# An attention and MoE kernel on one core: a fixed table of places for the first 820 operations, and another form of load for the second batch's queries

## The chip, the core and the metric

The kernel runs on one core of one Trainium2 chip. Its time is the device time of one execution in microseconds (us); the kernel before has a median of 866.38 us over three runs (864.64 to 868.58). The engines are PE (TensorE, with PEld for its weight loads), DVE (VectorE), ACT (ScalarE), POOL (GpSimd) and SP (SyncE), which here issues every DMA. Each engine works through its own instructions in the order in which the program has them; an instruction that waits holds up all that stand behind it on its engine.

## What is computed

```python
def _attn_ref(q, k, v):                        # q, k, v: 8 batches, 8 heads, 576 tokens, 64
    q_s = np.exp(q - np.max(q, axis=-1, keepdims=True))
    q_s = q_s / (np.sum(q_s, axis=-1, keepdims=True) + 1e-09)      # softmax over the 64
    k_s = np.exp(k - np.max(k, axis=2, keepdims=True))
    k_s = k_s / (np.sum(k_s, axis=2, keepdims=True) + 1e-09)       # softmax over the tokens
    kv = np.einsum('bhsd,bhse->bhde', k_s, v)
    return np.einsum('bhsd,bhde->bhse', q_s, kv)
...
x = attn_out.transpose(0, 2, 1, 3).reshape(4608, 512)
h = x @ w_in                                   # 512 x 2048
g = h * (1.0 / (1.0 + np.exp(-1.702 * h)))
out = g @ w_out                                # 2048 x 512
```

## The kernel before

The 4,608 tokens are cut into 12 tiles `t` of 384 (`TB`), three tokens to each of the 128 partitions. A batch has 576 tokens, so that tile 0 lies in batch 0, and tile 1 takes the last 192 tokens of batch 0 (on partitions 0 to 63) and the first 192 of batch 1 (on partitions 64 to 127). In float32 throughout, a product is made of three matmuls: each factor is split into a high part (`xh`, `gh`) and a low part (`xl`, `gl`).

**Attention.** `load_q`, `load_k`, `load_v` and `load_tail` load queries, keys, values and the last 64 tokens of keys and values, four heads (`i` = 0 or 1) at a time. `k_max` and `k_sub` make the keys' exponentials, `q_soft` the queries' softmax (DVE maximum L751, subtraction L755, ACT exponential L759, DVE sum L763, product L771 into `en`), `widen` (L428) copies the values, `kv_pairs` (PE L663) makes kv, `q_tr` (PE L793) transposes the queries, `x_pairs` (PE L876, L881) makes the attention's output x, and `x_out` (ACT L841, L853, PE L851, DVE L844) splits it. Batches 0 and 1 land in tiles of their own: `eq0`, `ek0`, `ev0`, `et` and `eq1`, `ek1`, `ev1`, `kl`, `vl`.

**MoE of tiles 0 and 1.** The loop runs over 16 slices `j` of the hidden layer. `g1` (PE L906, 12 matmuls of 128x384) makes h, ACT the gelu (L912) and its high part (L915), DVE the low part (L918), and `g2` (PE L938, nine matmuls of 128x512) adds to the output, which stays in PSUM. The weights come in as they are needed: `load_w` loads a slice or a pair of slices of `w_in` (`wi`, L316) or `w_out` (`wo`, L321), and `conv_w` (ACT L349 and L364, DVE L353, L357, L374) splits it.

**MoE of tiles 2 to 11.** They run in pairs as a Strassen-like product: seven products (`product`, PE L1180) and six parts of the output (`out_part`, PE L1244) for each step, with weights that `store` wrote to DRAM and `refill` brings back.

**What sets the order.** No loop of the program does. `Plan.add` records 2,604 operations with their engine, an assumed cost, what they read and write, and a rank; loads have a size as well. `Plan.order` then plays the program through with those assumed costs: an engine that is free takes the ready operation with the lowest rank, and loads share one wire of `RATE` bytes per us and land `LAND` us after it. The order in which operations begin is the order in which they are written out. The first 820 operations (those with a rank under `LIMIT`: attention of the first tiles, all weight loads, the MoE of tiles 0 and 1 and the first steps towards tiles 2 and 3) have their ranks replaced by the list `FIRST`, one number each:

```python
begun = [n for n, o in enumerate(plan.ops) if o[3] < LIMIT]
for n, r in zip(begun, FIRST):
    e, cost, deps, _, run, table, size = plan.ops[n]
    plan.ops[n] = e, cost, deps, r / 100, run, table, size
```

For the prediction these places matter: on SP the order of the loads (L519 queries, L439 keys, L453 values, L416 and L419 tails, L316 and L321 weights); on DVE and ACT the chains of `q_soft` for batch 1 between the steps that make x of tile 0; and on PE the first `g1` (L906), with which the MoE begins.

Of the kernel before, what the change touches and what calls it, by code (L numbers as in the profile page):

```python
# [17 lines left out]
class Plan:  # L18
# [4 lines left out]
    HOP, LAND, RATE, ISSUE, TABLE = 0.1, 2.2, 330e3, 0.6, 1.28  # L23
# [25 lines left out]
    def order(self):  # L49
        ops = self.ops  # L50
        left = [len(o[2]) for o in ops]
        users = [[] for _ in ops]
# [7 lines left out]
        at = [0.0] * len(ops)  # L60
# [7 lines left out]
        while len(began) < len(ops):  # L68
# [4 lines left out]
            for e in engines:  # L73
                if free[e] > now or not ready[e]:
                    continue
                _, n = heapq.heappop(ready[e])
                _, cost, _, _, _, needs, size = ops[n]
                if needs is not None and needs != table:
                    cost, table = cost + self.TABLE, needs
                free[e] = done = now + cost  # L80
                if size:
                    wire = max(wire, done) + size / self.RATE
                    done = wire + self.LAND
                began.append(n)
                self.start[n] = now
                moved = True
                for u in users[n]:
                    left[u] -= 1
                    hop = 0.0 if ops[u][0] == e and not size else self.HOP
                    at[u] = max(at[u], done + hop)  # L90
                    if not left[u]:
                        heapq.heappush(coming, (at[u], u))
# [76 lines left out]
def efficient_attention_then_gelu_ffn(  # L169
# [137 lines left out]
    def load_w(j, kind, rank):  # L307
# [16 lines left out]
        plan.add("SP", n * plan.ISSUE, (), (*keys, ("loaded", tags[0])), rank, run, size=n * 2 * DM * 4 * P)  # L324
# [82 lines left out]
    def load_tail(b, rank):  # L407
# [13 lines left out]
        plan.add("SP", plan.ISSUE, behind(b == 2), (keys[0],), rank, run_k, size=ST * H * D * 4)  # L421
# [1109 lines left out]
```

## Time and profile before

| what | value |
| --- | --- |
| median of three runs | 866.38 us (864.64 to 868.58) |
| the profiled execution's own time | 865.18 us |
| its span, first to last instruction | 863.4 us |
| PE busy (matmul), PEld | 838.8 us (97%), 735.5 us (85%) |
| DVE busy, ACT busy | 468.1 us (54%), 464.3 us (54%) |
| granted clock of PE, mean | 0.995 |
| DMA moved | 191.81 MB, mean 222 GB/s |

PE is busy for 97% of the span, which is a mean over stages: the views by stage stand in the prediction. A row of the timeline gives start, duration, engine, line, operation, tiles and, in brackets, how long the engine had been idle before it and what ended that. A row of the chain of waits gives start, duration and what the chain ran through. A row of the table of stretches gives the stretch and its length, then for PE, PEld, DVE, ACT and POOL the busy time and number of instructions, then the clock that PE was granted (1.00 is full), the mean busy share of the 16 DMA engines, and what they moved.

### The profile page before, as it was taken

The page shows a single profiled execution, that of the slowest core. Times are in us where ns is not written, and L with a number is a line of the kernel's source. Part 1 is how long each engine was busy: PE and PEld are TensorE (multiplying, and loading weights), DVE is VectorE, ACT ScalarE, POOL GpSimd, SP SyncE. Part 2 cuts the span into 40 slices and gives each one's busy share as a digit, 9 for nine tenths or more (in the row PEclk, how much of TensorE's full clock was granted, in tenths as well). Part 3 has the DMA queues.
Part 4 walks back from the last instruction along what each step waited for, and adds up shares of the span by engine and source line. Part 5 has one row for each costly group of instructions (what it writes and reads, how often), then busy time and mean ns, then how long its engine had stood idle before and what let it go on. Part 6 is the DMA issues. An engine that isn't in the chain of part 4 may idle for free.

```text
span 863.4 us, 12622 instructions
## 1 busy us (share of the span) xinstructions
PE 838.8 (97%) x4822; PEld 735.5 (85%) x4822; DVE 468.1 (54%) x791; ACT 464.3 (54%) x773; POOL 18.6 (2%) x21
## 2 busy tenths in 40 slices
PE   3799999999999999999999999999999999999998
PEld 2489998888888889888988888889888889888897
DVE  6789678886746573634476445557432434312212
ACT  6788558665536584564375465377423535423332
POOL 1000000000000000000000000000000000000000
PEclk9999999999999999999999999999999999999999
DMA  9997989729776658769547559656665455654522
GB/s 283 295 384 269 351 325 338 189 75 255 269 273 219 224 197 259 239 196 293 194 158 257 188 180 267 225 179 211 220 199 162 165 195 197 220 207 161 191 102 74
DMA packets 134924, 191.81 MB, mean 222 GB/s; under 512 B 65872, under 2 KB 97104, under 8 KB 134864
## 3 DMA queue, kind: packets, MB, share of 16 engines
q1 hardware_dynamic: 134864, 191.01, 68.2%
q8 instruction: 38, 0.62, 0.3%
q14 instruction: 22, 0.18, 0.1%
HBM read 154.21 MB, written 36.77 MB: 221 GB/s over the span
## 4 chain that ended last, share of the span: by engine, by line
PE 92%; DMA 4%; DVE 1%; SPq 1%; ACT 1%; issue 0%; POOL 0%; DVEq 0%; POOLq 0%
PE bank L1244 39%; PE bank L1180 33%; PE bank L938 8%; PE bank L906 7%; PE bank L793 2%; PE bank L881 2%; PE bank L663 2%; DMA eq<-in_q 1%; DMA ev<-in_v 1%; DMA kt<-in_k 1%; DMA ek<-in_k 1%; PE bank L876 1%; SPq L453 0%; SPq L1353 0%; DVE qm L763 0%
## 5 line engine op out<-in xcount | busy, mean ns | idle before, releaser
L1180 PE MATMUL bank<-xc,w 128*128 128x384 f32 x960 | 184.2, 337 | 0.0
L1180 PEld LDWEIGHTS bank<-xc,w 128*128 128x128 f32 x960 | 170.7, 188 | 8.6
L1244 PE MATMUL bank<-w,gp 128*128 128x512 f32 (+1 forms) x633 | 172.5, 396 | 0.0
L1180 PE MATMUL bank<-w 128*128 128x384 f32 x720 | 137.7, 337 | 0.4 <-DVE g L1196 0.4
L1244 PEld LDWEIGHTS bank<-w,gp 128*128 128x128 f32 x633 | 116.1, 188 | 24.9 <-issue 3.9
L1180 PEld LDWEIGHTS bank<-w 128*128 128x128 f32 x720 | 127.7, 188 | 3.8 <-DVE g L1196 0.7
L1244 PE MATMUL bank<-w,gh 128*128 128x512 f32 (+1 forms) x326 | 103.6, 399 | 0.0
L1244 PE MATMUL bank<-w 128*128 128x512 f32 x324 | 93.4, 396 | 0.0
L1215 ACT COPY bank<-bank 128x384 f32<-128x384 f32 x40 | 18.5, 463 | 129.1 <-PE bank L1180 129.1
L906 PE MATMUL bank<-xh,w 128*128 128x384 f32 x256 | 70.2, 339 | 0.0
L1244 PEld LDWEIGHTS bank<-w 128*128 128x128 f32 x324 | 59.8, 188 | 11.7 <-issue 0.6
L1244 PEld LDWEIGHTS bank<-w,gh 128*128 128x128 f32 x326 | 59.1, 188 | 12.1 <-issue 3.2
L1244 PE MATMUL bank<-w,gl 128*128 128x512 f32 (+1 forms) x163 | 64.0, 392 | 0.0
L938 PE MATMUL bank<-w,gh 128*128 128x512 f32 x192 | 62.2, 405 | 0.0
L906 PEld LDWEIGHTS bank<-xh,w 128*128 128x128 f32 x256 | 46.8, 188 | 2.2 <-issue 0.6
L1215 ACT COPY g<-bank 128x384 f32<-128x384 f32 x40 | 19.2, 479 | 49.5 <-PE bank L1180 49.3
L1215 ACT COPY work<-bank 128x384 f32<-128x384 f32 x40 | 19.2, 479 | 46.3 <-PE bank L1180 46.2
L906 PE MATMUL bank<-xl,w 128*128 128x384 f32 x128 | 43.2, 337 | 0.0
L938 PEld LDWEIGHTS bank<-w,gh 128*128 128x128 f32 x192 | 35.7, 191 | 5.6
L1211 DVE TENSOR_TENSOR gp<-work,gp 128x384 fp32r<-128x384 f32 x35 | 19.3, 555 | 35.0 <-ACT gp L1208 35.0
L938 PE MATMUL bank<-w,gl 128*128 128x512 f32 x96 | 38.1, 397 | 0.0
L1211 DVE TENSOR_TENSOR gp<-g,gp 128x384 fp32r<-128x384 f32 x35 | 19.7, 562 | 32.3 <-ACT gp L1208 32.3
(157 smaller groups left out, 1118.3 us busy)
## 6 DMA issues: line engine op xcount, KB each, us to landing
w<-dwo SPq DMA_DIRECT2D x80, 512.0 KB, 4.9
w<-dwi SPq DMA_DIRECT2D x44, 512.0 KB, 3.4
w<-dsh SPq DMA_DIRECT2D x32, 512.0 KB, 3.9
w<-dsl SPq DMA_DIRECT2D x32, 512.0 KB, 5.3
raw<-in_moe_w_in SPq DMA_DIRECT2D x16, 512.0 KB, 9.9
raw<-in_moe_w_out SPq DMA_DIRECT2D x16, 512.0 KB, 9.9
dwi<-w SPq DMA_DIRECT2D x16, 512.0 KB, 6.2
dwo<-w SPq DMA_DIRECT2D x16, 512.0 KB, 5.9
```

Source lines behind the costliest of these rows:

```text
L663: nc.tensor.matmul(pk[r0 : r0 + D, m, :], lhs, rhs, start=c == 0, stop=c == CM, tile_position=(0, r0))
L793: nc.tensor.transpose(pq[:, c * P : (c + 1) * P], qt[:, c, o : o + 2, :], ident)
L876: nc.tensor.matmul(po, kx, qx, start=True, stop=True)
L881: nc.tensor.matmul(po[ro], kx[ri, ro], qx[ri], start=fresh, stop=True, skip_group_check=True, tile_position=((a ^ odd) * D, a * D),)
L906: nc.tensor.matmul(ph, wi[w][j][:, c, :], x[:, c, :], start=c == 0 and i == 0, stop=c == KC - 1 and i == 2,)
L938: nc.tensor.matmul(po[c], x[:, cs], wo[w][j], start=j == 0 and i == 0, stop=j == NJ - 1 and i == 2)
L1180: nc.tensor.matmul(pb, ws[w][:, c * P : (c + 1) * P], xx[x][:, c * TB : (c + 1) * TB], start=p in FRESH and c == 0 and i == 0, stop=c == 1 ...
L1211: lambda: nc.vector.tensor_tensor(out=get()[1], in0=d, in1=get()[0].bitcast(F32), op=ALU.subtract),
L1215: plan.add("ACT", act(TB), (PB,), (key,), early_, lambda: nc.scalar.copy(dst, pb))
L1244: nc.tensor.matmul(po[:, f0:f1], x[:, cs], w[:, h * DM + f0 : h * DM + f1], start=m == 0 and e == 0 and i == 0, stop=m == NQ - 1 and e == ...
```

## The change

There are three parts.

**A table of places.** `FIRST` now holds the numbers 0 to 819, one place for each of the first 820 operations. They are sorted by it, and `order` gets the sorted list: of two operations on the same engine that follow each other in the list, the second may not begin before the first has. So each engine takes these operations in exactly the table's order. All other operations are still taken by rank whenever their engine is free and they are ready.

**Second batch's queries.** `load_q` for tile 1 loaded, for each half `i`, two blocks of 64 partitions by four heads by 192 values (one from batch 0, one from batch 1). Now it loads one head at a time over all 128 partitions, four loads for each half: the source is an access pattern written out by hand with two blocks of 64 rows (the step from the first to the second leads from batch 0's token 384 to batch 1's token 0 of the same head).

**Sizes and rates of the plan.** `RATE` rises from 330e3 to 395e3 and `LAND` falls from 2.2 to 2.1; the assumed size of `w_in`, keys and values grows by 1.17, that of queries by 1.1, tails have 1.8 of one tail's bytes each, and the two small loads of the identity three times theirs. These numbers only steer the order of the operations.

```diff
-    HOP, LAND, RATE, ISSUE, TABLE = 0.1, 2.2, 330e3, 0.6, 1.28
+    HOP, LAND, RATE, ISSUE, TABLE = 0.1, 2.1, 395e3, 0.6, 1.28
...
+        last, chain = {}, {}
+        for n in first:
+            e = ops[n][0]
+            if e in last:
+                chain[last[e]] = n
+                left[n] += 1
+            last[e] = n
...
-                for u in users[n]:
+                after = [(u, done + (0.0 if ops[u][0] == e and not size else self.HOP)) for u in users[n]]
+                if n in chain:
+                    after.append((chain[n], now))
+                for u, when in after:
                     left[u] -= 1
-                    hop = 0.0 if ops[u][0] == e and not size else self.HOP
-                    at[u] = max(at[u], done + hop)
+                    at[u] = max(at[u], when)
...
 FIRST = [
-    5378, -14100, -14622, -13398, -9246, -12627, -7965, -8342, -15809, -12626, -10477, -6145, -11454, -5989,
...
+    641, 3, 2, 4, 16, 12, 35, 5, 1, 0, 6, 22, 19, 14, 32, 42, 77, 34, 46, 24, 65, 87, 40, 74, 60, 69, 99, 80,
...
+            if t == 1:
+                for h in range(n):
+                    src = q[0:1, n * i + h, TB:S, :].rearrange("b (p c) d -> b p (c d)", c=C)
+                    step = [(H * S - TB) * D, 2]
+                    src = bass.AP(src.tensor, src.offset, [step, *list(src.ap)[1:]])
+                    nc.sync.dma_start(out=qt[:, h].rearrange("p c d -> p (c d)"), in_=src)
+                return
...
-    for n, r in zip(begun, FIRST):
+    first = sorted(begun, key=lambda n: FIRST[begun.index(n)]) if FIRST else []
+    for place, n in enumerate(first):
         e, cost, deps, _, run, table, size = plan.ops[n]
-        plan.ops[n] = e, cost, deps, r / 100, run, table, size
+        plan.ops[n] = e, cost, deps, place - 1e5, run, table, size
...
-        for n in plan.order():
+        for n in plan.order(first):
```

The line numbers in the changed program are other ones: L519 and L525 are loads of queries, L438 of keys, L452 of values, L414 and L417 of tails, L313 and L318 of weights; L757 to L777 is `q_soft`, L847 and L859 `x_out`, L912 `g1`.

**SP, the loads after the first batch's keys and values.** Before, the order of the loads from the eleventh on was this:

```order
L416 DMA kl0_107<-in_k 64x8x64
L321 DMA raw_218<-in_moe_w_out 128x1024
L439 DMA ek1_124<-in_k 128x4x256
L316 DMA raw_223<-in_moe_w_in 128x4x256
L453 DMA ev1_126<-in_v 128x4x256 x2
L419 DMA vl0_108<-in_v 64x8x64
L439 DMA ek1_124<-in_k 128x4x256
L321 DMA raw_235<-in_moe_w_out 128x1024
L519 DMA eq1_125<-in_q 64x4x192 x2
L316 DMA raw_247<-in_moe_w_in 128x4x256 x2
L519 DMA eq1_125<-in_q 64x4x192 x2
```

In the changed program stands there:

```order
L318 DMA raw_213<-in_moe_w_out 128x1024
L417 DMA et_129<-in_v 64x8x64
L313 DMA raw_219<-in_moe_w_in 128x4x256
L452 DMA ev0_123<-in_v 128x4x256
L519 DMA eq1_125<-in_q 128x1x192 x4
L438 DMA ek1_124<-in_k 128x4x256 x2
L313 DMA raw_265<-in_moe_w_in 128x4x256
L414 DMA kl0_107<-in_k 64x8x64
L519 DMA eq1_125<-in_q 128x1x192 x4
L313 DMA raw_293<-in_moe_w_in 128x4x256 x2
L452 DMA ev1_126<-in_v 128x4x256
```

The second batch's queries (`eq1`) come before its keys and values (`ek1`, `ev1`) and in eight loads instead of four; the first batch's keys and values (`ek0`, `ev0`) stay ahead of them, in both.

**ACT, the stretch in which x of tile 0 is finished.** Before, from the first of the last two `qT` on (the transposed queries; `xh0` and `xl0` are the high and low part of x of tile 0):

```order
L806 ACTIVATE qT2_101<-bank3_66,rb0_191 128x384
L853 CAST xl0_77<-bank0_63 128x384
L584 ACTIVATE ek1_124<-ek1_124 128x1024
L585 ACTIVATE kl0_107<-kl0_107 64x256
L841 CAST xh0_76<-bank3_66 128x384
L841 CAST xh0_76<-bank5_68 128x384
L853 CAST xl0_77<-bank3_66 128x384
L853 CAST xl0_77<-bank5_68 128x384
L759 ACTIVATE eq1_125<-eq1_125 128x768
L584 ACTIVATE ek1_124<-ek1_124 128x1024
L585 ACTIVATE kl0_107<-kl0_107 64x256
```

Now, up to the last `xl0`, the whole stretch from the first exponential of the second batch's queries on:

```order
L765 ACTIVATE eq1_125<-eq1_125 128x768
L705 COPY kvn0_74<-bank7_70 64x2x64
L347 ACTIVATE work0_84<-raw_265 128x512
L812 ACTIVATE qT2_101<-bank3_66,rb0_191 128x384
L812 ACTIVATE qT3_102<-bank4_67,rb0_191 128x384
...
L847 CAST xh0_76<-bank3_66 128x384
L362 CAST w_391<-work0_84 128x512
L859 CAST xl0_77<-bank3_66 128x384
L765 ACTIVATE eq1_125<-eq1_125 128x768
L347 ACTIVATE work2_86<-raw_293 128x1024
L859 CAST xl0_77<-bank5_68 128x384
```

Both exponentials of `eq1` and the conversion of a pair of `w_in` slices now stand ahead of the last `xl0`; the first `g1` reads all of `xh0` and `xl0`. The exponentials of `ek1`, one of which stood ahead, come after.

**DVE, the second half of those queries.** In the changed program these rows follow each other (`qm2` is the maximum over 64 values, L757 takes it, L761 subtracts it):

```order
L757 TENSOR_REDUCE qm2_195<-eq1_125 128x12
L559 TENSOR_TENSOR mx0_105<-tmp0_93 128x256
L355 SCALAR_TENSOR_TENSOR work0_84<-work0_84,raw_265 128x512
L562 TENSOR_TENSOR mx0_105<-mx0_105,kl0_107 64x256
L761 TENSOR_TENSOR eq1_125<-eq1_125,qm2_195 128x768
```

Before, the two halves' maxima stood after all keys of batch 1 had their maximum, with the steps of the other half between them:

```order
L751 TENSOR_REDUCE qm2_195<-eq1_125 128x12
L672 TENSOR_SCALAR rb1_192<-bank3_66 128x2
L673 RECIPROCAL rb1_192<-rb1_192 128x2
L755 TENSOR_TENSOR eq1_125<-eq1_125,qm2_195 128x768
L763 TENSOR_REDUCE qm3_196<-eq1_125 128x12
```

A conversion of weights (L355) and two steps of the keys' maximum moved in between the queries' maximum and subtraction.

More of the change, by code (lines that the diff above doesn't have):

```diff
@@ L47, in add, with order @@
         self.ops.append((engine, cost, deps, rank, run, table, size))
-    def order(self):
+    def order(self, first=()):
         ops = self.ops
         left = [len(o[2]) for o in ops]
+        last, chain = {}, {}
[5 more added lines that the diff above has]
+            last[e] = n
         users = [[] for _ in ops]
@@ L323, in load_w @@
         keys = [(tag, x) for tag in tags for x in (0, "v")]
-        plan.add("SP", n * plan.ISSUE, (), (*keys, ("loaded", tags[0])), rank, run, size=n * 2 * DM * 4 * P)
+        size = n * 2 * DM * 4 * P * (1.17 if kind == "wi" else 1)
+        plan.add("SP", n * plan.ISSUE, (), (*keys, ("loaded", tags[0])), rank, run, size=size)
     nt, nwork = [0], [0]
@@ L419, in run_v @@
             nc.sync.dma_start(out=vl[0:ST, :, 0:D], in_=v[b, :, SM:S, :].rearrange("h p d -> p h d"))
-        plan.add("SP", plan.ISSUE, behind(b == 2), (keys[0],), rank, run_k, size=ST * H * D * 4)
-        plan.add("SP", plan.ISSUE, behind(b == 2), (keys[1],), rank + 0.01, run_v, size=2 * ST * H * D * 4)
+        size = 1.8 * ST * H * D * 4
+        plan.add("SP", plan.ISSUE, behind(b == 2), (keys[0],), rank, run_k, size=size)
+        plan.add("SP", plan.ISSUE, behind(b == 2), (keys[1],), rank + 0.01, run_v, size=size)
     def widen(b, i, rank):
@@ L442, in run @@
             )
-        plan.add("SP", plan.ISSUE, behind(b == 2), (key,), rank, run, size=n * SM * D * 4)
+        plan.add("SP", plan.ISSUE, behind(b == 2), (key,), rank, run, size=1.17 * n * SM * D * 4)
     def load_v(b, i, rank):
@@ L463, in load_v @@
         if b < 2:
-            plan.add("SP", plan.ISSUE, (), (key,), rank, run, size=n * SM * D * 4)
+            plan.add("SP", plan.ISSUE, (), (key,), rank, run, size=1.17 * n * SM * D * 4)
             vbuf[b, i] = vt_[i], ("vt", i)
@@ L528, in load_q @@
         plan.add(
-            "SP", plan.ISSUE * len(parts(t)) * len(runs),
+            "SP", plan.ISSUE * (n if t == 1 else len(parts(t)) * len(runs)),
             behind(1 < t < EARLY_T) + after + (LOADED if t == EARLY_T else ()), (key, *alloc), rank, run,
-            size=n * TB * D * 4,
+            size=1.1 * n * TB * D * 4,
         )
@@ L1353, in ident_in @@
         nc.sync.dma_start(out=ident, in_=dident.rearrange("p f -> (p f)")[: P * P].rearrange("(p f) -> p f", p=P))
-    at(-100, lambda rank: plan.add("SP", plan.ISSUE, (), ("dident",), rank, ident_out, size=P * P * 4))
-    at(-89.2, lambda rank: plan.add("SP", plan.ISSUE, ("dident",), ("ident",), rank, ident_in, size=P * P * 4))
+    at(-100, lambda rank: plan.add("SP", plan.ISSUE, (), ("dident",), rank, ident_out, size=3 * P * P * 4))
+    at(-89.2, lambda rank: plan.add("SP", plan.ISSUE, ("dident",), ("ident",), rank, ident_in, size=3 * P * P * 4))
     at(-89.1, lambda rank: plan.add("ACT", act(P), ("ident",), ("minus",), rank, lambda: nc.scalar.mul(minus_r, ident, -1.0)))
```

88 rows, old and new, of the table FIRST are left out of this document.

## The prediction

> **What bounds the kernel now.** The page gives the whole first:
>
> ```profile
> span 863.4 us, 12622 instructions
> PE 838.8 (97%) x4822; PEld 735.5 (85%) x4822; DVE 468.1 (54%) x791; ACT 464.3 (54%) x773; POOL 18.6 (2%) x21
> ```
>
> PE lacks 24.6 us of the span. The table of stretches says where (columns: stretch, length, busy time of PE, PEld, DVE, ACT, POOL, granted clock, DMA share, GB/s):
>
> ```profile
> 10.00:20.00 10.00, 5.70 (x50) 4.52 (x51) 8.09 (x17) 6.63 (x12) 1.06 (x1) 1.00 1.11 308
> 20.00:30.00 10.00, 7.56 (x62) 4.08 (x61) 8.98 (x19) 8.77 (x18) 1.06 (x1) 0.96 1.11 298
> 30.00:40.00 10.00, 9.04 (x70) 6.82 (x70) 6.50 (x10) 6.43 (x13) 1.06 (x1) 0.87 1.10 284
> 40.00:50.00 10.00, 7.09 (x63) 6.18 (x64) 8.29 (x17) 7.83 (x16) 0.00 (x0) 0.83 1.06 386
> 50.00:60.00 10.00, 10.00 (x55) 9.06 (x55) 9.10 (x15) 9.89 (x17) 0.00 (x0) 1.00 1.04 387
> ...
> 220.00:863.00 643.00, 639.77 (x3567) 563.53 (x3565) 295.88 (x512) 311.93 (x535) 8.27 (x7) 1.00 0.62 204
> ```
>
> From 50 us on PE is full; the 3 us lacking after 220 are the usual seams, and neither part of the change touches them. What the change can move is the first 50 us, where PE waits and where the DMA engines never do: their share is above 1.0 from 10 us on, so all sixteen have packets in the queue all the time, and what lands later in the queue lands later by the price of what lands ahead of it. In the head the chain of waits (start, duration, what) runs through exactly these loads:
>
> ```profile
> 15.40 9.66 DMA ev<-in_v
> ...
> 26.09 10.98 DMA eq<-in_q
> ...
> 41.89 0.97 DVE en L771
> ...
> 42.91 1.54 PE bank L793 x6
> ```
>
> and three moments of the timeline show what it costs there:
>
> ```profile
> 33.68 0.69 PE L663 MATMUL bank<-vt,ek 128*64 128x65 f32 x16
> 33.78 0.48 ACT L853 CAST xl<-bank 128x384 fp32r<-128x384 f32 x1 [0.15 <-PE bank L851]
> ...
> 35.00 0.45 PE L906 MATMUL bank<-xh,w 128*128 128x384 f32 x1
> ...
> 42.91 1.33 PE L793 MATMUL bank<-ident,en 128*128 128x128 f32 x5 [3.48 <-DVE en L771]
> ```
>
> The first `g1` begins at 35.00, straight after `kv_pairs` of batch 1 (33.68 to 35.00, 1.3 us). The last `xl0` that it needs was there at 34.26. It works until 42.91 - 3.48 = 39.43, so 4.4 us, and then stops for 3.48 us for `en`, the queries of tile 1, whose second half is the load that ends the 10.98 us, at 37.07. So the end follows from a simple sum: all PE work from the first `g1` on is given, and the end is the **start of the first `g1`**, plus this work, plus what PE idles behind that start (3.48 us).
>
> **The change, part by part.** The plan's sizes and rates cost the chip nothing; they act through the order alone. Whether the table is obeyed is seen in the order rows above: it is. What remains is how the loads are made and what now stands ahead of the first `g1`.
>
> *The price of a new load.* What before pays for queries:
>
> ```profile
> eq<-in_q SPq DMA_DIRECT2D x2, 384.0 KB, 4.3
> eq<-in_q SPq DMA_DIRECT2D x4, 192.0 KB, 9.9
> ...
> 18.70 0.43 DVE L353 TENSOR_SCALAR raw<-raw 128x512 uint32<-128x512 uint32 x1 [0.20 <-DMA raw<-in_moe_w_out]
> ```
>
> Half of tile 1's queries is 384 KB (393,216 bytes), formerly two loads of 64 rows, now four of 128. Bytes alone don't set the price: the stretches with the 64-row loads move 284 and 298 GB/s, the one from 40 to 50, in which only 128-row loads of weights go, 386. No load in the trace is written like the new one. Every load of before has an outermost dimension of 64 or more on both sides, and its stretches show sixteen busy engines. The new one's source is two blocks, each of 64 rows: its outermost dimension is 2. So the cost is bounded from both sides. If the sixteen engines share it, half the queries cost 393,216 / 386e3 = 1.0 us to 393,216 / 298e3 = 1.3 us. If the rows are dealt out by the outermost dimension, two engines carry it all. One engine moves 386/16 = 24.1 to 308/16 = 19.3 GB/s; 393,216 bytes over two take 8.2 to 10.2 us (11.1 at 284). By rows alone the price is anywhere from 1.0 to 11.1 us, and the nearest row, the 64-row load, lies at the cheap end. I nevertheless take the dear end, 9.2 us, the mean of 8.2 and 10.2, since the outermost dimension is the one thing in which these loads differ from all that use sixteen engines.
>
> The Trainium skill bears on this, "DMA: Bandwidth & Descriptors", section "Why a DMA increments its semaphore by 16 and not by 1": a transfer uses the largest number of engines up to 16 that divides the slowest dimension over 1 on either side, as the instruction carries it. For 2 and 128 this is two engines, the dear end; by any sharing over sixteen it would be the cheap one. The loads of before, all multiples of 16 there, agree with their DMA share of 1.06 to 1.11; the case of two engines no run here shows.
>
> *When the queries land.* In before the first `wo` has landed by 18.70. Ahead of the new loads stand the same loads without `kl` (128 KB, 0.4 us at 308 GB/s; as a 64-row load more, I take 0.8), so they begin at **17.9**. First half: 17.9 + 9.2 = 27.1. Then `ek1` twice, a `w_in` slice and `kl`, 1.70 MB, 4.4 us at 386 and 5.5 at 308 GB/s, taken as 5.0: 32.1. The two engines have their sixteenths of these to carry as well, so being alone saves them nothing. Second half: **41.3** (38.7 with all quick ends, 45.6 with 11.1 and 5.5). SP has four more issues to make; at 0.96 us (one in before's chain, wait included) that is 3.8 us, and it runs 9.9 us ahead of the landing, so this hides; if it didn't, 3.8 us would be the price.
>
> *What stands behind them.* The groups by line, operation and shape (busy, mean ns of one | idle before it):
>
> ```profile
> L751 DVE TENSOR_REDUCE qm<-eq 128x12 f32<-128x768 f32 x4 | 3.8, 946 | 6.7 <-DMA eq<-in_q 6.7
> L755 DVE TENSOR_TENSOR eq<-eq,qm 128x768 f32<-128x768 f32 x4 | 3.8, 949 | 0.1
> L553 DVE TENSOR_TENSOR mx<-tmp 128x256 f32<-128x256 f32 x16 | 6.7, 422 | 0.3
> L556 DVE TENSOR_TENSOR mx<-mx,kl 64x256 f32<-64x256 f32 x14 | 5.7, 415 | 0.6 <-DMA kl<-in_k 0.2
> L357 DVE SCALAR_TENSOR_TENSOR work<-work,raw 128x512 int32<-128x512 int32 x4 | 2.8, 689 | 0.6 <-ACT work L349 0.5
> L759 ACT ACTIVATE eq<-eq 128x768 f32<-128x768 f32 x4 | 3.4, 845 | 1.6 <-DVE eq L755 1.6
> L349 ACT ACTIVATE work<-raw 128x1024 f32<-128x1024 f32 x14 | 15.9, 1152 | 0.9 <-ACT w L364 0.9
> L853 ACT CAST xl<-bank 128x384 fp32r<-128x384 f32 x4 | 1.9, 476 | 0.2 <-PE bank L851 0.2
> L428 ACT COPY vt<-ev 128x1024 f32<-128x1024 f32 x4 | 4.2, 1053 | 2.5 <-DMA ev<-in_v 2.5
> L584 ACT ACTIVATE ek<-ek 128x1024 f32<-128x1024 f32 x3 | 3.2, 1056 | 0.0
> L585 ACT ACTIVATE kl<-kl 64x256 f32<-64x256 f32 x14 | 5.6, 401 | 0.0
> ```
>
> From the second half's landing on DVE does, in the order of the rows above, maximum, L553, L357, L556 and subtraction: 0.95 + 0.42 + 0.69 + 0.42 + 0.95 = 3.43 us. ACT then has the exponential, the conversion of a `w_in` pair and the last `xl0`, which stand in a row: 0.85 + 1.15 + 0.48 = 2.48. With 0.2 us of hops the first `g1` starts at 41.3 + 3.4 + 2.5 + 0.2 = **47.4**. Nothing shortens this: each engine keeps its order, and tile 0's x, long since computed by PE, waits behind tile 1's queries.
>
> *The sum.* First `g1` 35.0 to 47.4: +12.4. `kv_pairs` of batch 1 now comes behind it: +1.3. The wait of 3.48 for `en` goes: before, the last `en` ended 5.8 us after its landing (42.86 - 37.07), now with the two steps between some 7.3 later, at 48.6, and PE has `g1` until 47.4 + 4.4 = 51.8: -3.5. What is late next is the stalls behind the new start, none to 2.5 us (gelu, keys and values of batch 1, which land after 41); I take 1.3. Sum **+11.5**, bounds from +7.6 (38.7, no stall) to +17.0 (45.6, 2.5). The half clock neither gains nor loses:
>
> ```profile
> 43.00:46.00 3.00, 3.00 (x11) 2.61 (x12) 2.90 (x4) 2.64 (x7) 0.00 (x0) 0.50 1.07 394
> ```
>
> After its 3.48 us of idling PE is granted 0.50 for some 3 us, which costs 1.5; behind the longer wait of the new kernel the same is due once.
>
> The profiled execution took 865.18 us and the median is 866.38, 1.2 more. So 865.2 + 11.5 = 876.7 for the profile, and **877.9** for the median, own range 874 to 883.
>
> **Rivals.** *A: sixteen engines share the new loads, and the table does what it is for* (not slower). Landings: 17.9 + 1.2 = 19.1 and, 5 + 1.2 us later, 25.3. The second half is then 11.8 us sooner than at 37.07, and no `en` is waited for. ACT sets the first `g1`: ahead of it go two copies L428, one exponential of `ek1` and one of `kl` (2 x 1.05 + 1.06 + 0.40 = 3.56 us), and come two of `eq1` and a pair's conversion (2 x 0.85 + 1.15 = 2.84): 0.7 less. The last `xl0` is there at 34.26 - 0.7, and with `kv_pairs` no longer ahead the first `g1` starts then, at 33.6. Sum: -1.4 + 1.3 - 3.5 + 1.1 for new waits (0 to 3.5) = -2.5, which gives 863.9, 861.5 to 866. For it: the stretches of before show nothing but full sharing. Against it: the outermost dimension. It decides from a price per half below about 3 us; above, the landing sets the start.
>
> *C: sixteen engines, but dear.* Each new load costs what a 64-row load of 192 KB did, 1.3 us and more, so 5 us a half: first half 23, second 33. Then the first `g1` starts at 33 + 6.1 = 39, +4.1 + 1.3 - 3.5 + 1 = +2.9, near 869. For it: 284 GB/s in the 64-row stretches. Against it: the new loads fill 128 rows.
>
> *D: the fixed order alone is the trouble*: a strict order on ACT and DVE makes an early instruction wait for a late one, as DVE already waits 6.7 us at L751. Without dear loads it costs A's gain at most, near 867; I count it with C.
>
> **How the numbers follow.** The forecast, two engines: 0.68. A: 0.20. C and D: 0.12. The predicted time is the forecast's, 878. The range has to reach from the forecast's upper bound, 883, down until 8 in 10 are held: the forecast's own range holds some 0.6 of its 0.68, C and D bring it to 0.7, and of A the greater part is needed, so 863. A measurement of this kernel tells 0.5% from no change, 862.0 and 870.7. The forecast lies above wholly, with a tenth of C and D: 0.69 slower. A lies within but for its lower end, and so do C and D for the most part: 0.25 the same; faster 0.06, a quarter of A and a little for a better order than I see.
>
> **What would show it.** The queries' maxima on DVE: each waits for `eq`, the first till about 27, the second till about 41 (A: 19 and 25). The DMA share in those two stretches falls well below 1 where before it is 1.1; were it above 1 at 300 GB/s, the forecast is wrong at its first step. The first `g1` stands at 47 (A: 34; C: 39), behind an ACT that waits for the exponential. Behind it PE has no wait of 3.5 us for `en` any more, and after 60 us the tables of stretches are alike but for the shift. If the loads lie behind the other fourteen engines' work without holding it up, and something else, say `ev1`, sets the end, then the landing is right and the sum is not.

## The result, and the profile after

The changed kernel takes 876.8 us (median of 6 runs, 874.9 to 880.63), the kernel before 866.29 in as many runs: 1.0123 times as long, with a 95% interval of 1.0098 to 1.0147. The profiled execution took 875.92 us, 10.7 more than that of before. The changed kernel's page begins so:

```profile
span 874.1 us, 12625 instructions
...
PE 841.9 (96%) x4822; PEld 736.1 (84%) x4822; DVE 466.4 (53%) x791; ACT 456.2 (52%) x767; POOL 25.6 (3%) x21
```

PE does the same 4,822 matmuls and stands still for 32 us instead of 25. The table of stretches (columns as in the prediction) answers line by line to that of before:

```profile
10.00:20.00 10.00, 8.04 (x54) 4.18 (x55) 8.80 (x19) 7.19 (x13) 2.87 (x2) 1.00 0.72 207
20.00:30.00 10.00, 4.32 (x52) 3.17 (x51) 4.06 (x7) 3.89 (x9) 0.00 (x0) 0.83 0.68 191
30.00:40.00 10.00, 7.28 (x19) 4.07 (x18) 2.35 (x6) 4.07 (x9) 1.06 (x1) 0.66 0.44 119
40.00:50.00 10.00, 4.00 (x12) 4.00 (x13) 9.08 (x13) 6.55 (x10) 2.74 (x1) 0.51 1.04 329
50.00:60.00 10.00, 10.00 (x89) 9.23 (x88) 9.62 (x18) 9.95 (x19) 0.00 (x0) 0.98 1.08 351
...
220.00:874.00 654.00, 648.27 (x3615) 569.26 (x3614) 301.20 (x524) 317.43 (x543) 7.46 (x7) 1.00 0.62 203
```

Look at the last two columns from 10 to 40 us: the DMA share was 1.1 there, and is 0.72, 0.68 and 0.44 now; the rate fell from some 300 GB/s to as little as 119. From 20 to 40 us PE, DVE and ACT are also busy for less time than before, since their data is not there. Finer stretches, in which hardly anything but tile 1's queries lands, show the price of the new loads bare:

```profile
17.00:21.00 4.00, 4.00 (x15) 1.97 (x16) 2.83 (x9) 3.48 (x8) 0.00 (x0) 1.00 0.14 43
31.00:36.00 5.00, 4.33 (x10) 2.24 (x8) 1.34 (x4) 3.10 (x8) 1.06 (x1) 0.50 0.14 43
```

The share is 0.14 and the rate 43 GB/s. Stretches with all sixteen engines at work show a share of 1.11, and two sixteenths of that are 0.14. The trace also records the counts by which the engines that carry a load report their part as landed: the first of the new loads gets two of them at its end, at 18.56 and 18.61 us (a single one stands right behind the issue, at 11.84). A half of tile 1's queries, 393,216 bytes, takes 393,216 / 43e3 = 9.1 us at this rate. The timeline shows the two landings by the maximum on DVE that waits for each, then `en` at 51.25, and PE's first `g1` (an instruction's start and duration, and in brackets its engine's idle time before):

```profile
25.87 0.95 DVE L757 TENSOR_REDUCE qm<-eq 128x12 f32<-128x768 f32 x1 [5.89 <-DMA eq<-in_q]
...
36.82 0.34 PE L912 MATMUL bank<-xh,w 128*128 128x384 f32 x1
...
40.61 0.95 DVE L757 TENSOR_REDUCE qm<-eq 128x12 f32<-128x768 f32 x1 [8.26 <-DMA eq<-in_q]
...
46.00 0.69 PE L912 MATMUL bank<-xl,w 128*128 128x384 f32 x1 [7.79 <-ACT xl L859]
...
51.25 0.96 DVE L777 TENSOR_TENSOR en<-eq,qm 128x768 f32<-128x768 f32 x1
```

And the chain of waits through the head (start, duration, what) runs from the second half's loads to the dense part:

```profile
31.03 9.45 DMA eq<-in_q
...
42.82 0.88 DVE eq L761
...
44.47 0.41 ACT work L347
...
45.49 0.47 ACT xl L859
...
46.00 5.23 PE bank L912 x17
51.23 1.32 PE bank L669 x40
52.55 0.81 PE bank L799 x6
```

The three stations that the prediction named stand there one behind the other: the load, the subtraction on DVE, the pair's conversion and the last `xl0` on ACT. PE began the first `g1` at 36.82, did seven matmuls with what it had, and waited 7.79 us for that `xl0`. PE's waits from 46 us on are these (total in us, times, longest). The second block is the whole list of before, from 43 us on:

```profile
PE bank L912 <- ACT xl L859: 7.8, 1, 7.8
PE bank L1186 <- DVE g L1202: 1.2, 2, 1.0
PE bank L1186 <- DVE qT L820: 0.6, 1, 0.6
PE bank L887 <- DVE work L1202: 0.6, 1, 0.6
```

```profile
PE bank L793 <- DVE en L771: 3.5, 1, 3.5
PE bank L1180 <- DVE g L1196: 0.4, 1, 0.4
```

The last three of the first block add up to 2.4 us and lie behind 60 us, in a part that the prediction held to be untouched. An experiment below looks at them.

### The profile page after: what moved, and what is told of

Same layout as the page of the kernel before. It is cut to its first block, busy times and chain, and to the rows that moved or that the text cites. A ratio compares the mean times of both kernels' runs of the same rounds, so it can differ in the third digit from the quotient of the medians.

```text
span 874.1 us, 12625 instructions
## 1 busy us (share of the span) xinstructions
PE 841.9 (96%) x4822; PEld 736.1 (84%) x4822; DVE 466.4 (53%) x791; ACT 456.2 (52%) x767; POOL 25.6 (3%) x21
## 4 chain that ended last, share of the span: by engine, by line
PE 88%; DMA 5%; SPq 3%; DVE 2%; issue 1%; ACT 0%; POOL 0%; DVEq 0%; POOLq 0%
PE bank L1250 36%; PE bank L1186 31%; PE bank L912 8%; PE bank L944 8%; PE bank L669 2%; DMA kt<-in_k 2%; PE bank L799 2%; SPq L519 2%; PE bank L887 2%; DMA eq<-in_q 1%; DMA out<-tmp 1%; DMA kl<-in_k 1%; DMA dident<-spread 1%; PE bank L882 1%; SPq L438 0%
## 5 line engine op out<-in xcount | busy, mean ns | idle before, releaser
L912 PE MATMUL bank<-xh,w 128*128 128x384 f32 x256 | 70.8, 346 | 0.0
L912 PE MATMUL bank<-xl,w 128*128 128x384 f32 x128 | 44.3, 346 | 7.8 <-ACT xl L859 7.8
L912 PEld LDWEIGHTS bank<-xh,w 128*128 128x128 f32 x256 | 48.2, 194 | 1.3 <-issue 0.6
L566 POOL PARTITION_ALL_REDUCE mx<-mx x16 | 24.9, 1554 | 523.4 <-DVE mx L562 520.2
```

The lines of the kernel that those rows point to most:

```text
L566: nc.gpsimd.partition_all_reduce(flat, flat, P, bass_isa.ReduceOp.max)
L912: nc.tensor.matmul(ph, wi[w][j][:, c, :], x[:, c, :], start=c == 0 and i == 0, stop=c == KC - 1 and i == 2,)
```

## The experiments

The theory: the source of the new loads has an outermost dimension of 2, so two DMA engines carry each of them, and this is the whole loss. Its rivals: the fixed order holds ACT and DVE up; a load is dear because it is small, or one of many; any source of more than one block is dear. In every run the line numbers shift a little with the edit.

**The old loads under the new order, and the new loads under the old.** The first takes the branch for tile 1 out of the changed `load_q`; order and plan are those of the changed kernel.

```diff
-            if t == 1:
-                for h in range(n):
...
-                    nc.sync.dma_start(out=qt[:, h].rearrange("p c d -> p (c d)"), in_=src)
-                return
```

> The changed kernel with its table and its plan, but each half of tile 1's queries loaded as before, as two loads of 64 rows by four heads. Theory (the two-block source puts a load on two DMA engines, and that is the whole loss): the halves land near 19 and 26 us instead of 26 and 40, PE's wait of 7.8 us for the last xl0 is gone, all twelve matmuls of the first g1 run from about 33.6, and the time is 863.9 us (861.5 to 866), so 2 to 3 us under the kernel before. Rival (the fixed order alone holds ACT and DVE up): the wait for xl0 stays in part and the time stays above 867.

Measured: 864.59 us (12 runs), 0.9981 of before (0.9968 to 0.9994). The 12 us between this and the changed kernel are the loads; the order by itself gains a little. One wait for `xl0` is left, where the expectation had none; it is 1.9 us and not 7.8. This is PE's list of waits from 30 us on in this kernel:

```profile
PE bank L1179 <- DVE g L1195: 2.3, 1, 2.3
PE bank L905 <- ACT xl L852: 1.9, 1, 1.9
PE bank L792 <- DVE en L770: 1.0, 1, 1.0
...
PE bank L1179 <- DVE qT L813: 0.6, 1, 0.6
```

The queries landed a little later than expected (the maxima start at 21.0 and 29.0, not after 19 and 26), and the rest of the first `g1` began at 34.4 rather than 33.6.

The second puts the same branch into the kernel before.

> The kernel before with its own order, and only the loads of tile 1's queries in the new form. Theory: each half costs 9.1 us at 43 GB/s instead of some 3, so the second half lands near 51 instead of 37.07 and PE's wait of 3.48 us for en grows by 14; the time is about 880 us (875 to 886). Rival (the order is what costs): 866, within 2 us.

Measured: 879.1 us, 1.0142 (1.0124 to 1.0161). PE's timeline has one long gap, at the place that the kernel before waited 3.48 us:

```profile
56.52 1.54 PE L800 MATMUL bank<-ident,en 128*128 128x128 f32 x6 [16.67 <-DVE en L778]
```

The wait grew by 13.2 us, where 14 were expected. So the loads cost as much under the old order (12.3 us) as under the new (12.2): the rival of the order falls.

**The same rows under another outermost dimension.** Two kernels wrote the old loads of 64 rows as 2 x 32 and as 4 x 16 rows.

```diff
+                    rows, *rest = [list(x) for x in src.ap]
+                    m = rows[1] // 2
+                    src = bass.AP(src.tensor, src.offset, [[rows[0] * m, 2], [rows[0], m], *rest])
```

> The changed kernel with two loads of 64 rows by four heads for each half, the same rows and bytes as in the kernel before; only the source is written as 2 x 32 rows instead of 64, so that its outermost dimension is 2. Theory (the outermost dimension decides): the same as the changed kernel, 43 GB/s while these loads run and 875 to 879 us. Rival (the number of loads, their 96 KB, or a source that spans two batches decides): as with the old loads, 862 to 866 us.

> As the kernel with 2 x 32 rows, but the source written as 4 x 16 rows. Theory: four engines, 86 GB/s, so a half costs 4.6 us instead of 9.1 and the second half lands 9 us earlier than in the changed kernel, near 31.5; the first g1's last matmuls start near 37 instead of 46 and the time is about 868 us (866 to 871). Rival: any outermost dimension under 16 costs the same, 876; or none matters, 864.

Measured: 864.09 us (0.9975, 0.9964 to 0.9986) and 864.7 us (0.9971, 0.9955 to 0.9986), the time of the old loads. This tells nothing against the theory, since the experiments missed their aim: the steps are even, 32 rows of 192 values make exactly the step of the next block, and the instruction in the built program has one dimension of 64 again. All three kernels are one program, and its time is known the better for it.

What can't be folded is a source with gaps. The next two keep the changed kernel's loads, one for each head over 128 partitions, and take the rows from blocks with a gap between them: four of 32 rows, and sixteen of 8 (there the last line has a step of `10 * C * D` and 16 blocks of 8 rows). With other tokens their output is another, so they measure loads and do not replace the kernel.

```diff
-                    src = q[0:1, n * i + h, TB:S, :].rearrange("b (p c) d -> b p (c d)", c=C)
-                    step = [(H * S - TB) * D, 2]
-                    src = bass.AP(src.tensor, src.offset, [step, *list(src.ap)[1:]])
+                    src = q[0:1, n * i + h, 0 : P * C, :].rearrange("b (p c) d -> b p (c d)", c=C)
+                    src = bass.AP(src.tensor, src.offset, [[40 * C * D, 4], [C * D, 32], [1, C * D]])
```

> The changed kernel's four loads of 128 rows for each half, but the source is four blocks of 32 rows with a gap of 8 rows between them (it can't be folded into one run), so its outermost dimension is 4. The rows come from other tokens, so tile 1's queries, and with them its part of the output, are others. Theory: four engines, 86 GB/s, 4.6 us a half instead of 9.1; the second half lands 9 us earlier than at 40.5, the last xl0 comes near 37, and the time is 867 us (865.5 to 869.5). Rival (a source of several blocks is dear whatever their number): 875 to 879.

> As the kernel with four blocks, but sixteen blocks of 8 rows with gaps of 2, outermost dimension 16; tile 1's queries are again of other tokens. Theory: sixteen engines, a half costs 1.0 to 1.3 us, the DMA share stays above 1, and the time is that of the kernel with the old loads or a little less, 862 to 865.5 us. Rival as before: 875 to 879, or in between if the number of loads has a price of its own.

Measured: 868.39 us (1.0019, 1.0008 to 1.0031) and 862.97 us (0.9955, 0.994 to 0.9969). A stretch of the first, while its second half comes in, and one of the second, around its first half:

```profile
27.00:28.00 1.00, 0.00 (x0) 0.00 (x0) 1.00 (x4) 0.91 (x2) 0.00 (x0) 1.00 0.28 80
```

```profile
16.00:20.00 4.00, 4.00 (x41) 2.52 (x38) 3.12 (x10) 2.82 (x6) 0.00 (x0) 1.00 1.11 287
```

Share and rate about double from two blocks to four (0.14 to 0.28, 43 to 80 GB/s), and with sixteen all engines are at work. The counts of landed parts say the same: at its end the first of these loads gets two, four and sixteen of them. The starts of the two maxima on DVE bear on what a half costs, in the list of the instructions that touch `eq`; these are the changed kernel's, the four blocks' and the sixteen blocks' rows (durations, then first and last start):

```profile
L757 DVE TENSOR_REDUCE qm<-eq x2: 952/952/953, 25.9 to 40.6; 128x12 f32<-128x768 f32 x2
```

```profile
L756 DVE TENSOR_REDUCE qm<-eq x2: 953/953/953, 22.3 to 32.9; 128x12 f32<-128x768 f32 x2
```

```profile
L756 DVE TENSOR_REDUCE qm<-eq x2: 945/950/954, 20.3 to 27.2; 128x12 f32<-128x768 f32 x2
```

They lie 14.7, 10.6 and 6.9 us apart. The last is a little short: with sixteen blocks DVE was still at other work when the first half landed, and the landings themselves lie 7.4 us apart (19.8 and 27.1). A half costs 9.1, 4.9 and 1.4 us at the rates shown (393,216 bytes at 43, 80 and 287 GB/s). Less these, 5.6, 5.7 and 6.0 are left, which is the price of the four loads in between, and nearly the same in all three. The rival that several blocks are dear whatever their number falls. By the rule in the Trainium skill's "DMA: Bandwidth & Descriptors", section "Why a DMA increments its semaphore by 16 and not by 1", the number of engines is the largest up to 16 that divides both slowest dimensions over 1; the runs agree with it at 2, 4 and 16. How far the blocks lie from each other was not varied by itself.

**Twice as many loads, half as large.** Every head's load is cut in its two blocks.

```diff
                 for h in range(n):
-                    src = q[0:1, n * i + h, TB:S, :].rearrange("b (p c) d -> b p (c d)", c=C)
...
+                    for b, s0, p0, p1 in parts(t):
+                        src = q[b, n * i + h, s0 : s0 + (p1 - p0) * C, :].rearrange("(p c) d -> p (c d)", c=C)
+                        nc.sync.dma_start(out=qt[p0:p1, h].rearrange("p c d -> p (c d)"), in_=src)
```

> The changed kernel with every head's load cut in its two blocks of 64 rows: 8 loads of 48 KB for each half, twice as many as in the changed kernel and half as large, each with an outermost dimension of 64. Theory (the outermost dimension decides): all sixteen engines share them, the DMA share is above 1 where it fell to 0.11 to 0.2; four issues more a half on SP, 0.6 us each, cost some 2.5 us a half at most: 864 to 869 us. Rival (many small loads are what is dear): slower than the changed kernel, above 877.

Measured: 866.49 us, 0.9992 (0.9977 to 1.0007). Twice the number of loads is 10 us quicker than the changed kernel, so the number isn't what is dear. Half of the expectation missed, though: the DMA share did not stay above 1.

```profile
17.00:21.00 4.00, 4.00 (x22) 1.90 (x19) 3.23 (x9) 3.17 (x7) 0.00 (x0) 1.00 0.35 75
```

One reason lies on SP, in the list of what touches `eq` (shortest, median and longest ns of one issue):

```profile
L518 SPq DMA_DIRECT2D eq<-in_q x10: 465/594/1029, 16.0 to 26.4; - x10
```

At 0.594 us for 49,152 bytes SP can issue some 83 GB/s. But that is not the whole of it: the stretch is uneven (72, 4, 71 and 152 GB/s in its four microseconds), and SP's waits from 16 to 30 us include 2.1 us for earlier loads of `w_in` and 1.4 us for `ev`, before it issues more of these. How the shortfall divides was not tested. The cost against the old loads, 1 to 2 us, is not clear of the noise (the intervals against the kernel before overlap); against the sixteen blocks, timed beside it, it is 3.5 us.

**The table without the plan's new numbers.** The kernel before with the table and the code that obeys it; sizes, `RATE` and `LAND` as before, loads as before. Until about 200 us all engines have the same order as with the old loads above.

```diff
-    HOP, LAND, RATE, ISSUE, TABLE = 0.1, 2.1, 395e3, 0.6, 1.28
+    HOP, LAND, RATE, ISSUE, TABLE = 0.1, 2.2, 330e3, 0.6, 1.28
...
-        plan.add("SP", plan.ISSUE, behind(b == 2), (key,), rank, run, size=1.17 * n * SM * D * 4)
+        plan.add("SP", plan.ISSUE, behind(b == 2), (key,), rank, run, size=n * SM * D * 4)
...
```

> The kernel before with the table of places alone: loads and the plan's sizes and rates as before. The first 820 operations stand in the same order as with the old loads in the changed kernel; what follows (from about 200 us on) is ordered by the old numbers. Theory (the waits of 2.7 to 3.4 us that PE has there in the changed kernel with the old loads, against 0.4 before, come from the new numbers): these waits fall under 1 us and the time is 862.5 us (861 to 864). Rival (they come from the table): the time stays at 864.5 within 0.7.

Measured: 861.98 us, 0.9947 (0.9933 to 0.9962), the quickest kernel of the study, and 2.6 us under the one with the new numbers. PE's waits from 30 us on show where: the head's are there much as they were, and of the later ones (3.4 us with the old loads above: L1179 with 2.3 + 0.6, and 0.5 in a row not shown) one of 1.1 us is left, where the expectation had under 1:

```profile
PE bank L903 <- ACT xl L850: 2.2, 1, 2.2
PE bank L660 <- DMA vl<-in_v: 1.1, 1, 1.1
PE bank L1177 <- DVE g L1193: 1.1, 1, 1.1
PE bank L790 <- DVE en L768: 0.7, 1, 0.7
```

So the new numbers give, behind the last operation that the table holds, an order that costs some 2 us. The two kernels were timed in different sessions, each beside the kernel before; their intervals against it (0.9968 to 0.9994, 0.9933 to 0.9962) don't overlap. The size is less sure than the sign: the three profiles of the one program with the old loads show 2.3 to 3.4 us of these later waits, and the sixteen blocks, with the new numbers and in the session of the table alone, took only 1.0 us more than it, with intervals that overlap.

**Tile 0's x ahead of tile 1's queries.** On the changed kernel, and on the table alone, the last two `xl0` were put ahead of the conversion and the exponential in front of them.

```diff
     first = sorted(begun, key=lambda n: FIRST[begun.index(n)]) if FIRST else []
+    for n in (94, 90):
+        first.remove(n)
+        first.insert(first.index(113), n)
```

> The changed kernel with one edit to the order on ACT: the last two xl0 go ahead of the conversion L362 and of the exponential of the second half of tile 1's queries, so that tile 0's x no longer waits for these queries. The loads stay on two engines. What the prediction's step says (the end is set by the first g1, which waits behind tile 1's queries on ACT): PE's wait of 7.8 us for xl0 goes, the first g1 runs through near 37, and 3 to 7 us are saved: 870 to 874 us. The other reading (the landing of the queries sets the end anyway, through en and through the conversion of the next w_in slice, which stands behind their maximum on DVE): the wait only moves to the second g1 and to q_tr, and no more than 1 us is saved: 875.5 to 877 us.

> The same edit on the kernel before with the table alone, which was the quickest so far (862.0 us). PE waits 2.2 us for the last xl0 there. If en comes next at an unchanged time, the wait moves to en: 861 to 862.5 us. If the wait is a loss of its own: 859.5 to 860.5 us.

Measured: 876.34 us (1.0109, 1.0089 to 1.013) and 862.1 us (0.9939, 0.992 to 0.9958): no gain that can be measured in either. In the first, PE's list of waits from 30 us on now begins:

```profile
PE bank L912 <- ACT w L362: 3.7, 1, 3.7
PE bank L912 <- DVE w L372: 3.0, 1, 3.0
...
PE bank L799 <- DVE en L777: 0.2, 1, 0.2
```

The 7.8 us for `xl0` have become 6.7 for the next slice of `w_in`, whose conversion stands behind the maximum of the late queries on DVE. The transposes of `en` then begin at 52.66 us, after a wait of 0.2, where they began at 52.55 in the changed kernel: `en` would have held PE until then anyway. The late landing reached PE by three ways of about the same length; taking one of them away changes nothing. In the second kernel the 2.2 us for `xl0` became 2.1 for the next slice of `w_in` too, and not, as expected, a wait for `en`, which stayed at 0.7.

| kernel | outermost dimension of the loads | GB/s meanwhile | maxima start at | us |
| --- | --- | --- | --- | --- |
| changed | 2 | 43 | 25.9, 40.6 | 876.8 |
| four blocks | 4 | 80 | 22.3, 32.9 | 868.4 |
| sixteen blocks | 16 | 287 | 20.3, 27.2 | 863.0 |
| old loads | 64 | 298 (20 to 30 us) | 21.0, 29.0 | 864.6 |
| table alone | 64 | 295 (20 to 30 us) | 21.0, 28.7 | 862.0 |

## Why the prediction was right, and where its steps were not

The forecast was 877.9 us with 9.2 us for a half; measured were 876.8 and 9.1. The mechanism was right; that the total came so near is in part luck, since two errors of opposite sign offset each other, as the sum below shows.

- **What bounds the kernel.** Right for the head. Wrong for the rest: "neither part of the change touches them" was said of the waits behind 60 us, but the plan's numbers order everything behind the first 820 operations, and PE's waits there went from 0.4 to 2.4 us (with the table alone they are 1.1). This step failed by argument, not by size: that numbers "act through the order alone" was said, and then the order that they make was looked at only in the head.
- **The price of a new load.** Right: two engines, 43 GB/s, 9.1 us. The experiments with four and sixteen blocks bear out the reason, the outermost dimension.
- **When the queries land.** 25.9 and 40.6 against 27.1 and 41.3. The first loads began some 1.1 us sooner than the 17.9 assumed (25.9 - 9.1 = 16.8); the loads in between took 5.6, not 5.0.
- **What stands behind them.** 5.4 us from the second landing to the last `xl0`'s successor (40.61 to 46.00), against 6.1. But the first `g1` is not one block: seven of its matmuls ran at 36.8, so that what began at 46.00 was worth a start at 44.8 (seven times 0.17 us earlier).
- **Nothing waits for `en` any more.** The wait is gone from the list, but not for the reason given. `en` was put at 48.6; it ended at 52.2, 0.35 us before PE's transposes began (52.55). The step left out what else DVE has in between (two subtractions L582, the keys' tails L587 and three steps of weight conversion). The last `g1` before them ended near 51.2, so only `kv_pairs` of batch 1, 51.23 to 52.55, covered `en`: that no wait came is luck as well. Had `xl0` been earlier, the next slice of `w_in` and right behind it `en` would have held PE, as the kernel with `xl0` first shows (6.7 and 0.2 us).
- **The half clock.** "Neither gains nor loses" was a little off: after 7.8 us of idling the grant stayed at 0.50 longer than in before. The first two rows are the changed kernel's, the last follows the prediction's row of 43 to 46 us in before:

```profile
46.00:50.00 4.00, 4.00 (x12) 4.00 (x13) 3.90 (x6) 3.27 (x5) 0.00 (x0) 0.50 1.08 282
50.00:52.00 2.00, 2.00 (x34) 1.75 (x35) 1.90 (x4) 1.98 (x3) 0.00 (x0) 0.90 1.04 362
```

```profile
46.00:48.00 2.00, 2.00 (x44) 1.57 (x42) 0.68 (x2) 1.19 (x2) 0.00 (x0) 0.94 1.01 404
```

That is 4.4 us at half speed (4.0 and a fifth of 2.0), 2.2 us lost, against 3.2 us (3.0 and 0.12 of 2.0) and 1.6 lost in before.

The sum in measured terms: 44.8 - 35.0 = +9.8 for the start, +1.3 for `kv_pairs`, -3.5 for `en`, +0.6 for the clock, +2.0 for the later waits, together +10.2 of the 10.7 by which the spans differ. In the prediction these were +12.4, +1.3, -3.5, 0 and +1.3. The prediction had the start 2.6 us too late and the rest 1.3 too cheap, so that the total of 11.5 was nearer than its parts. Its 1.3 us for stalls were meant for gelu, keys and values right behind the new start, and no such wait stands in the list; the 2.0 us are the later waits, which it did not foresee.

The rival A (all sixteen engines, 863.9) is what the kernel with the old loads shows: 864.6. The rival C, 64-row prices for the new loads, holds for no kernel here; D, the order alone, is excluded.

## What to carry to other kernels

Look at the outermost dimension on both sides of a load before looking at its bytes: here a source of two far blocks, written as one access pattern to fill all 128 partitions, ran at a seventh of the rate of two loads of 64 rows. When a fixed order ends somewhere, what comes behind it is still made by the old rules, and a change to their numbers has to be priced there as well. And a wait that is the longest on the list is worth its length only if no other path ends just behind it: here a wait of 7.8 us was taken away, and nothing that can be measured was gained.

## What the runs showed of the hardware that was not expected

While the two engines were at work, the other fourteen were idle for about half of the time (17 to 21 and 31 to 36 us above), and SP was slow to issue what comes next. SP's timeline of the changed kernel, and then of the one with the old loads, at the issues of the two halves:

```profile
10.83 7.67 SPq L519 DMA_DIRECT2D eq<-in_q  x4
18.55 3.55 SPq L438 DMA_DIRECT2D ek<-in_k  x2
...
24.61 8.67 SPq L519 DMA_DIRECT2D eq<-in_q  x4
```

```profile
11.09 1.26 SPq L518 DMA_DIRECT2D eq<-in_q  x2
...
19.70 2.22 SPq L518 DMA_DIRECT2D eq<-in_q  x2
```

Four loads held SP for 7.67 and 8.67 us, two of the old form, of the same bytes together, for 1.26 and 2.22. It goes by the engines, not by the number of loads: four loads from four blocks held SP for 4.20 and 6.13 us, four from sixteen blocks for 2.63 and 2.86. So a load on few engines holds back the loads behind it at the issue already. What SP waits for in that time the trace doesn't name. Once the next loads are issued, the others' engines do run ahead, as the prediction's last section thought possible, while the two are still busy; the halves land only at 25.8 and 40.5 us:

```profile
23.00:26.00 3.00, 0.06 (x3) 0.00 (x0) 0.13 (x1) 0.26 (x1) 0.00 (x0) 1.00 0.81 232
38.00:41.00 3.00, 0.20 (x2) 0.00 (x0) 0.39 (x1) 0.00 (x0) 0.00 (x0) 0.86 0.94 260
```

The rate of one engine was 21.5 GB/s with two at work, 20 with four, and 18 with sixteen (287 / 16). The last is a mean over all loads of its stretch, not over the new ones alone.
